# A gated pair of 2-D spectral filters: the last two row transforms on halves of the TensorE array

## The chip, the cores and the metric

The kernel runs on one core of a Trainium2 chip. The metric is the device time of one execution in microseconds. Before the change it is 122.04 us, the median of three runs (122.02 to 122.52).

## The reference

`x` has 2048 rows of 1024 values (bf16). Both branches filter the same `x`; they differ only in their complex weights. The gate is one number for each row.

```python
X = rfft2(x.astype(float32), axes=(-2, -1))          # 2048 x 513, complex
a = irfft2(X * (A_w_r + 1j * A_w_i), s=(2048, 1024)).astype(bfloat16)
b = irfft2(X * (B_w_r + 1j * B_w_i), s=(2048, 1024)).astype(bfloat16)
g = sigmoid((x * gate_w).sum(-1, keepdims=True))
return g * a + (1 - g) * b
```

## The kernel before, in words

All transforms are matmuls with constant matrices. A row transform of length 2048 is done as 32 times 64, a column transform of length 1024 as one real matrix whose symmetry halves the work ("folding": even and odd parts are multiplied apart, and the sum and the difference of the results give the two mirrored halves).

The stages, with the line of their matmul in the profile: stage 1 (L387) does the 32-part of the forward row transform, stage 2 (L456, L465) the forward column transform, stage 4 (L482) the 64-part of the forward row transform. VectorE multiplies by the weights (`product`, L505); the real and imaginary parts of a spectrum sit on alternate partitions, and the copy with the parts swapped is made by a DMA inside SBUF.

Stage 5 (`group_mm`, L614) does the 64-part of the inverse row transform. It works on 256 column indices `l0`, 8 of them in a group. For each, two matmuls (one for each of the tiles WB and WA) accumulate in PSUM: the stationary operand is 128 columns of the products, taken from the tile at a stride of half a slot (264 or 257 elements), so that its columns run slot by slot and, within a slot, over the two halves of the spectrum's columns. The moving operand is a 128-column constant. The result has a PSUM partition for each (slot, half). A group fills two PSUM banks and is copied back to WB in one go, by ScalarE (`group_out`, L625), a few by VectorE (L623). Four pairs of banks are used in turn.

In the middle of stage 5 the gate is made: `row_sums` (VectorE, L533 to L537) ends in AB, `zsum` (L561) spreads AB over the partitions by matmuls, and ScalarE takes the sigmoid (L564). `gate_mask` (L570) then makes two masked copies of the gates, zero on the partitions of the other half, and `rbgen` (L601) multiplies them into the constants of stage 6: 16 row blocks of 1024 elements each on a partition. Twelve of these products are made in stage 5 and four among stages 6 and 7.

Stage 6 (`stage6_mm`, L755) does the 32-part of the inverse row transform and the gated sum of both branches in one contraction over 128 partitions (branch, slot, half). Because the halves must not be mixed, the moving constant has 2 x 32 output columns for every output kind, one set for each half, with zeros where the partition belongs to the other half. A row block takes 16 matmuls of 128 moving columns, and one copy of 1024 columns by ScalarE (L770) to the tile of Y.

Stage 7 (`stage7`, L785) does the inverse column transform of one row block of 128 rows. A folded block takes 8 matmuls of 256 columns; ScalarE copies the even part (L792), VectorE makes sum and difference in f32 (two L832), GpSimd adds and subtracts again and writes bf16 (two L837), and a DMA stores the block. A "full" block uses twice the columns in each matmul (8 of 512) and needs only the copy and two VectorE operations (L796). A "half" block unfolds one part: 4 matmuls of 256 and 4 of 512 columns, four VectorE operations (L818, L796), no GpSimd.

The order of work on each engine is the order of the `P.add` calls; a small planner turns the keys of what is read and written into semaphores, and sets no times. Stage 6 of block r + 2 is issued ahead of stage 7 of block r, with PSUM banks 0 and 1 or 6 and 7 for stage 6 and 2 to 5 for stage 7. Four f32 buffers for VectorE's sums (`NPQ`) stand between it and GpSimd. Stores are issued by SP, two of the last by ScalarE.

Of the kernel before, what the change touches and what calls it, by code (L numbers as in the profile page):

```python
# [6 lines left out]
ALU = mybir.AluOpType  # L7
AP = bass.AP
# [3 lines left out]
RWS = (528, RW)  # L12
# [13 lines left out]
def make_consts():  # L26
# [22 lines left out]
    row = np.arange(128)  # L49
# [4 lines left out]
    F2 = []  # L54
    for cmb, par in ((0, 0), (1, 1), (2, 1), (3, 0)):
# [5 lines left out]
        else:  # L61
            F = F[0].reshape(128, 2, 2, 32, 2)
            e = [np.stack([F[:, :, 0, :, w], F[:, :, 1, :, 1 - w]], axis=2).reshape(128, 128) for w in range(2)]
# [28 lines left out]
    c, s = np.cos(pi2 * kk * o2 / 64), np.sin(pi2 * kk * o2 / 64)  # L92
# [4 lines left out]
    e = np.eye(64)  # L97
# [9 lines left out]
    blocks += [m[perm][:, perm] for m in (T1, T3, -T3, T3z, -T3z, T2, T4, -T4, T4z, -T4z)]  # L107
    C["CL"] = np.concatenate([VR, MK.reshape(128, 64)] + blocks, axis=1)

    l2, sl_, f = row % 2, (row // 2) % 32, row // 64  # L110
    k1 = K1_OF[sl_]
    U5 = np.zeros((128, 16, 2, 2, 4, 32))
    o1 = np.arange(32)[None, :]
# [5 lines left out]
    C["U5"] = U5.reshape(128, 8192)  # L119
    SM = np.zeros((128, 4), np.float32)  # L120
    SM[:, 0] = np.where(f == 0, 1.0, -1.0)
    SM[:, 1], SM[:, 2] = l2 == 0, l2 == 1
    C["SM"] = SM
    DI = np.zeros((128, 2, 2, 2, 512))
    d = np.arange(512)[None, :]
    for pi in range(2):
        for h in range(2):
# [5 lines left out]
            a = pi2 * l * (d + 0.5) / 1024  # L133
# [101 lines left out]
def bass_gated_mix__spectral_gfnet__spectral_gfnet__prompt_kernel(nc, A_x, A_w_r, A_w_i, B_x, B_w_r, B_w_i, gate_w, out):  # L235
# [7 lines left out]
    WA = sb("WA", 64 * RW)  # L243
    WB = sb("WB", 64 * RWS[0])
    FT = sb("FT", 16384)
    XF = sb("XF", 9216)
    MM = sb("MM", 6144)
    F2 = sb("F2", 2048)
    EO = sb("EO", 1024)
    W5 = sb("W5", 64)  # L250
    CK = sb("CK", C["CK"].shape[1])
    CL = sb("CL", C["CL"].shape[1])
# [6 lines left out]
    SM = sb("SM", 4, f32)  # L259
    GRo = 1024  # L260
    DUM = sb("DUM", 2, f32)
    PS = nc.alloc_psum_tensor("PS", [128, 4096], f32)
    WT = (WB, WA)

    def sl(t, off, dims, p0=0, np_=128, pstep=1):
        n = t.shape[1]
        return AP(t, p0 * n + off, [[n * pstep, np_]] + [list(x) for x in dims])

    def ps(col, dims):
        return AP(PS, col, [[4096, 128]] + [list(x) for x in dims])  # L270

    def bank(b):
        return ("ps", b)
# [279 lines left out]
                  r=["XST", "XSS", ("W5", 0), ("W5", 1)], a=["PST"])  # L553


    GMo = lambda r: (XF, 7168 + r * 256) if r < 8 else (MM, 4096 + (r - 8) * 256)

    def zsum(us):
        for k, u in enumerate(us):
            for n in range(16):  # L560
                P.add("pe", lambda e, n=n, u=u, k=k: e.matmul(ps(u * 1024 + 64 * n, [(1, 64)]), sl(AB, 16 * k + n, [(0, 128)]), sl(CL, MKo, [(1, 64)]),  # L561
                                                              start=True, stop=True),
                      r=["AB", "CV"], w=[bank(2 * u + n // 8)])
            P.add("act", lambda e, u=u, k=k: e.activation(sl(XF, 16 * k, [(32, 64), (1, 16)]), ps(u * 1024, [(1, 64), (64, 16)]), ACT.Sigmoid, scale=SM[:, 0:1]),  # L564
                  r=[bank(2 * u), bank(2 * u + 1), "SM"], **({"a" if k else "w": [("CS", 0), ("CS", 1)]}))

    def gate_mask(hf):
        t, o = GMo(8 * hf)
        for h in range(2):
            P.add("dve", lambda e, h=h: e.tensor_scalar(  # L570
                out=sl(t, o + h * 32, [(64, 32), (1, 32)]), in0=sl(XF, 1024 * hf, [(32, 32), (1, 32)]),
                scalar1=SM[:, 1 + h:2 + h], scalar2=None, op0=ALU.mult),
                r=[("CS", hf), "SM"], w=[("GM", hf, h), ("XS" if hf else "X", 4), ("XS" if hf else "X", 5)])


    def col0(u, sw):
# [14 lines left out]
              r=[bank(bk)], w=[("col0", sw)])  # L591

    U5o, DIo = 0, 1024
    RBS = [(FT, (4 + k) * 2048 + 1024, []) for k in range(4)] + [(F2, 1024 * k, ["F2"]) for k in range(2)]
    RBS += [(XF, 1024 * k, [("CS", k)]) for k in range(3)] + [(XF, 3072 + 1024 * k, [("X", k)]) for k in range(4)]
    RBS += [(MM, 1024 * k, [("XS", k)]) for k in range(4)]

    def rbgen(r, eng, after=()):
        t, o, k = RBS[r]
        g, go = GMo(r)  # L600
        return P.add(eng, lambda e: e.tensor_tensor(  # L601
            out=sl(t, o, [(256, 4), (64, 4), (32, 2), (1, 32)]),
            in0=sl(FT, U5o + (r // 2) * 2048 + (r % 2) * 512, [(128, 4), (32, 4), (0, 2), (1, 32)]),
            in1=sl(g, go, [(0, 4), (64, 4), (32, 2), (1, 32)]), op=ALU.mult),
            r=["U5", ("GM", r // 8, 0), ("GM", r // 8, 1)], w=[("RB", r)] + k, after=[last2] + list(after))

    def group_mm(u, g, qs, at):
        hf = g // 16
        for q in qs:
            l0 = 8 * g + q  # L610
            o = ps(u * 1024 + at(q) * 128, [(1, 128)])
            for ab in range(2):
                deps = [("prod", ab, hf, g // 8 % 2), "CL"] + [("col0", ab)] * (g == 0)
                P.add("pe", lambda e, o=o, l0=l0, ab=ab: e.matmul(  # L614
                    o, sl(WT[ab], l0, [(RWS[ab] // 2, 128)]), sl(CL, KIo[ab], [(1, 128)]), start=(ab == 0), stop=(ab == 1)),
                    r=deps, w=[bank(2 * u + at(q) // 4)])

    def group_out(u, g, eng, q0, n, st, at, keys):
        src = ps(u * 1024 + at * 128, [(1, 128), (128, n)])
# [104 lines left out]
    for n, g in enumerate(range(16, 32)):  # L724
        if n == 14:
            last_groups([spare(), spare()])
        elif n < 14:
            group(spare(), g, "dve" if n == 1 else "act")
        if n == 1:
            zsum([spare(), spare()])  # L730
            gate_mask(0)
            gate_mask(1)
            for _ in range(12):
                rbgen(rb.pop(0), "dve")
    assert slots[-2:] == [1, 2]
    last5 = P.ops["pe"][-1]
# [8 lines left out]
    def stage6_mm(r, bs, pis):  # L745
        b0 = 6 * (r % 2)
        t6, o6, _ = RBS[r]
        for b in bs:
            for pi in pis:
                for cp in range(2):  # L750
                    n = cp * 64 + 16 * b + r
                    lh = sl(WB, n * (RWS[0] // 2) + pi, [(2, 128)])
                    rh = sl(t6, o6 + cp * 512 + b * 64, [(256, 2), (1, 64)])
                    o = ps(b0 * 512 + b * 256 + pi * 128, [(1, 128)])
                    P.add("pe", lambda e, o=o, lh=lh, rh=rh, cp=cp: e.matmul(o, lh, rh, start=(cp == 0), stop=(cp == 1)),  # L755
                          r=[("Z", pi), ("RB", r)], w=[bank(b0 + b // 2)])

    def stage6(r, mm=True):
        b0 = 6 * (r % 2)
        if mm:  # L760
            stage6_mm(r, range(4), range(2))
        for k in range(2 if r == 0 else 1):
            n = 2 if r == 0 else 4
            src = ps((b0 + k) * 512, [(32, 8), (1, 32), (256, n)])
            dst = sl(WA, Yo + r * 128 + 2 * k, [(2048, 8), (4, 32), (1, n)])
            kw = dict(r=[bank(b0 + k + q) for q in range(n // 2)], a=[("Y", r)], after=[last5])
            if r == k == 0:
                P.add("dve", lambda e, s=src, d=dst: e.tensor_copy(d, s), **kw)  # L768
            else:
                P.add("act", lambda e, s=src, d=dst: e.activation(d, s, ACT.Copy), **kw)  # L770

    HALF = (5, 9, 12)
    pqc = 0

    def stage7(r):
        nonlocal pqc
        full, half = r >= 14, r in HALF
        b0 = 6 * (r - 14) if r >= 14 else 4 - 2 * (r % 2)
        oo = OUo + (r % NOU) * 1024
        es = sl(WA, EOo + (r % 2) * 1024, [(1, 1024)]).bitcast(f32)  # L780

        def mm(col, c0, n, ri, pi, h, k, last):
            lh = sl(WA, Yo + (pi * 4 + ri * 2 + h) * 2048 + r * 128, [(1, 128)])
            rh = sl(FT, DIo + pi * 2048 + (ri * 2 + h) * 256 + c0 * 4096, [(4096, n), (1, 256)])
            P.add("pe", lambda e: e.matmul(ps(col, [(1, n * 256)]), lh, rh, start=(k == 0), stop=(k == last)),  # L785
                  r=[("Y", r), "DI"] + ["DJ"] * (full or half), w=[bank(col // 512)])
# [14 lines left out]
        if full:  # L801
            for k in range(4):
                mm((b0 + 1) * 512, 0, 2, 1, k // 2, k % 2, k, 3)
            even(0, 512)
            for k0, n, bk in ((0, 2, b0),) if r == 14 else ((0, 1, b0), (1, 1, 4)):
                for k in range(4):
                    mm(bk * 512, k0, n, 0, k // 2, k % 2, k, 3)
                finals(k0, n, bk, WA, EOo + (r % 2) * 1024, [("EO", r % 2)])
        elif half:
# [7 lines left out]
            for s, op in enumerate((ALU.add, ALU.subtract)):  # L817
                P.add("dve", lambda e, s=s, op=op: e.tensor_tensor(out=sl(MM, to + s * 512, [(1, 512)]).bitcast(f32),  # L818
                                                                   in0=ps((b0 + 1) * 512, [(1, 256)]), in1=es[:, :256], op=op),
                      r=[("EO", r % 2), bank(b0 + 1)], w=[("T", r % 2, s), ("GM", 1, 0), ("GM", 1, 1)])  # L820
            finals(0, 2, b0, MM, to, [("T", r % 2, 0), ("T", r % 2, 1)])
        else:
            for e_ in (1, 0):
# [28 lines left out]
    stage6_mm(1, range(2, 4), (0,))  # L852
    stage6_mm(1, range(4), (1,))
    stage6(1, False)
    for _ in range(3):
        rbgen(rb.pop(0), "dve")
    for r in range(16):
        for q in {0: (), 1: (2,), 2: (3, 4)}.get(r, (r + 2,) if r < 14 else ()):
            stage6(q)
        late += stage7(r)  # L860
        if rb:
            rbgen(rb.pop(0), "dve")
        if r < 13:
            outs.append(late.pop()())
    outs += [late[k]() for k in (1, 2, 0, 3)]
# [62 lines left out]
```

## Time and profile before

| | us |
|---|---|
| median of three runs | 122.04 |
| the profiled execution | 122.14 |
| its span | 120.1 |
| PE busy (95% of the span), 1556 matmuls | 114.1 |
| VectorE busy (83%) | 99.5 |
| ScalarE busy (82%) | 99.0 |
| GpSimd busy (32%) | 38.4 |
| stage 5, L614: first start to the last stage 5 matmul | 49.76 to 84.1 |
| stages 6 and 7, L755 and L785 | 84.02 to 115.9 |
| granted TensorE clock, mean | 0.996 |

A PE busy time is the union of pipelined matmul records, each of which lasts longer than its share of the array: a 128-column matmul is shown with 219 ns, while such matmuls start 55.6 ns apart. So the price of a matmul is read from starts, or from the pieces of the chain that ended last, and not from its own duration. Up to 50 us the chain runs over the loading of the weights (SP's queue, 18% of the span; a weight DMA, 9%) and the last products; from there on it is PE for all but the tail.

### The profile page before, as it was taken

Reading aid. Unit: us, or ns where it says so; the run is one execution under the profiler, and the core shown is the slowest. Engines: PE = TensorE matmul, PEld = TensorE weight load, DVE = VectorE, ACT = ScalarE, POOL = GpSimd, SP = SyncE. Lnnn points to the kernel's source line nnn. Section 1 sums busy time; section 2 is a strip of 40 time slices with the busy share of each in tenths; the row PEclk is TensorE's granted clock in tenths of the full one; section 3 lists DMA queues with packets and bytes.
Section 4 is the critical chain, followed back from the end, with each engine's and each line's share of the span. In section 5 each row is a group of like instructions: output and inputs, shape, how many; then the busy total and the mean of one; then the engine's idle time right before and its main releaser. Section 6 shows DMA issues by size and latency. Waiting matters only on the chain.

```text
span 120.1 us, 3690 instructions
## 1 busy us (share of the span) xinstructions
PE 114.1 (95%) x1556; PEld 95.9 (80%) x1556; DVE 99.5 (83%) x160; ACT 99.0 (82%) x119; POOL 38.4 (32%) x47
## 2 busy tenths in 40 slices
PE   6998999999999999999999999999999999999960
PEld 4676889787675675689999999999899979898630
DVE  0568999988999999999999949995695687787890
ACT  4249998999797999899999989999779868867710
POOL 1000010036575500000000000000029999999980
PEclk9999999999999999999999999999999999999998
DMA  2999999999999999832699500000000422434456
GB/s 84 328 394 421 415 331 366 349 350 352 361 369 364 360 370 368 321 137 85 162 392 394 199 0 5 0 5 0 0 5 8 158 96 93 175 124 160 160 222 215
DMA packets 17680, 26.11 MB, mean 217 GB/s; under 512 B 2112, under 2 KB 11072, under 8 KB 17664
## 3 DMA queue, kind: packets, MB, share of 16 engines
q1 hardware_dynamic: 16368, 23.00, 54.6%
q0 software_dynamic: 864, 2.36, 5.4%
q10 hardware_dynamic: 432, 0.52, 1.4%
q8 instruction: 12, 0.20, 0.7%
q14 instruction: 4, 0.03, 0.1%
HBM read 17.48 MB, written 4.19 MB: 180 GB/s over the span
## 4 chain that ended last, share of the span: by engine, by line
PE 59%; SPq 18%; DMA 9%; DVE 8%; issue 3%; ACT 1%; POOL 0%; DVEq 0%; POOLq 0%
PE PS L614 26%; SPq L290 18%; PE PS L785 14%; PE PS L755 11%; DMA WA<-in_B_w_i_dram 9%; DVE WA L505 3%; PE PS L304 3%; DVE WB L505 3%; PE PS L387 2%; DVE WA L796 1%; PE PS L561 1%; PE PS L482 1%; PE PS L588 1%; ACT WB L625 1%; DVEq L867 0%
## 5 line engine op out<-in xcount | busy, mean ns | idle before, releaser
L837 POOL TENSOR_TENSOR WA<-WA 128x512 bf16<-128x512 f32 x22 | 27.6, 1290 | 48.2 <-DVE WA L832 48.2
L614 PE MATMUL PS<-CL,WB 128*128 128x128 bf16 x256 | 31.8, 226 | 0.0
L614 PE MATMUL PS<-CL,WA 128*128 128x128 bf16 x256 | 31.7, 223 | 0.1
L614 PEld LDWEIGHTS PS<-CL,WB 128*128 128x128 bf16 x256 | 31.3, 145 | 0.3 <-DVE WB L505 0.2
L614 PEld LDWEIGHTS PS<-CL,WA 128*128 128x128 bf16 x256 | 31.3, 145 | 0.3 <-DVE WA L505 0.2
L625 ACT ACTIVATE WB<-PS 128x1024 bf16<-128x1024 f32 (+1 forms) x31 | 28.8, 1042 | 0.2 <-PE PS L614 0.2
L770 ACT ACTIVATE WA<-PS 128x1024 bf16<-128x1024 f32 (+1 forms) x16 | 15.8, 996 | 6.2 <-PE PS L755 6.1
L505 DVE TENSOR_TENSOR WB<-XF,WA 128x2048 bf16<-128x2048 bf16 (+2 forms) x14 | 19.3, 1384 | 1.0 <-ACT XF L490 0.5
L785 PE MATMUL PS<-FT,WA 128*128 128x256 bf16 (+1 forms) x132 | 19.3, 292 | 0.1
L505 DVE TENSOR_TENSOR WA<-MM,WA 128x2048 bf16<-128x2048 bf16 (+2 forms) x14 | 19.2, 1385 | 0.0
L482 PE MATMUL PS<-XF,CK 128*128 128x512 bf16 (+1 forms) x72 | 17.5, 356 | 0.2 <-ACT XF L490 0.2
L832 DVE TENSOR_TENSOR WA<-PS,WA 128x512 f32<-128x512 f32 x22 | 14.2, 686 | 4.2 <-PE PS L755 1.9
L471 ACT ACTIVATE XF<-PS 128x1024 bf16<-128x1024 f32 x16 | 16.7, 1052 | 1.1 <-PE PS L465 1.0
L490 ACT ACTIVATE XF<-PS 128x1024 bf16<-128x1024 f32 x14 | 14.7, 1050 | 1.4 <-PE PS L482 0.6
L387 PE MATMUL PS<-MM,XF 128*128 128x256 bf16 x128 | 15.4, 280 | 0.3 <-DVE XF L348 0.3
L387 PEld LDWEIGHTS PS<-MM,XF 128*128 128x128 bf16 x128 | 12.5, 100 | 3.3 <-DVE XF L348 1.4
L785 PEld LDWEIGHTS PS<-FT,WA 128*128 128x128 bf16 x132 | 12.3, 98 | 3.3 <-DVE WA L768 0.2
L290 POOL DMA_DIRECT2D MM<-XF x18 | 9.9, 550 | 14.3 <-PE PS L482 8.7
L398 ACT ACTIVATE FT<-PS 128x1024 bf16<-128x1024 f32 (+2 forms) x15 | 13.1, 1012 | 0.9 <-PE PS L387 0.9
L348 DVE TENSOR_TENSOR XF<-WB 128x512 bf16<-128x512 bf16 (+1 forms) x20 | 6.0, 366 | 5.9 <-DMA WB<-in_A_x_dram 5.9
L456 PEld LDWEIGHTS PS<-F,FT 128*128 128x128 bf16 x128 | 8.4, 98 | 3.1 <-ACT FT L398 0.2
L456 PE MATMUL PS<-F,FT 128*128 128x128 bf16 x128 | 10.2, 219 | 0.0
(77 smaller groups left out, 134.1 us busy)
## 6 DMA issues: line engine op xcount, KB each, us to landing
out_dram<-WA SPq DMA_DIRECT2D x14, 256.0 KB, 2.2
MM<-XF POOLq DMA_DIRECT2D x18, 128.0 KB, 5.3
WA<-in_A_x_dram SPq DMA_DIRECT2D x4, 512.0 KB, 8.3
FT<-c_U SPq DMA_DIRECT2D x1, 2048.0 KB, 8.5
MM<-XF SPq DMA_DIRECT2D x14, 128.0 KB, 3.2
WB<-in_A_x_dram SPq DMA_DIRECT2D x3, 512.0 KB, 5.9
WA<-in_A_w_r_dram SPq DMA_DIRECT2D x4, 256.5 KB, 5.8
WA<-in_A_w_i_dram SPq DMA_DIRECT2D x4, 256.5 KB, 6.2
```

The costliest lines, as they stand in the source:

```text
L290: return P.add(eng, lambda e: e.dma_start(dst, src), dma=name, **kw)
L387: P.add("pe", lambda e, o=o, lh=lh, rh=rh, s=s: e.matmul(o, lh, rh, start=(s == 0), stop=(s == 1)), r=[("xf", c % 2, q, h, s ^ j), ("M", c ...
L456: P.add("pe", lambda e, o=o, cs=cs, j=j, t=t, rh=rh: e.matmul(o, fblock(1 + cs, j, t), rh, start=(j == 0), stop=(j == 1)), r=[("F1a" if p ...
L471: P.add("act", lambda e: e.activation(dst, src, ACT.Copy), **kw)
L482: P.add("pe", lambda e, o=o, kind=kind, pm=pm, m=m, rh=rh: e.matmul(o, sl(CK, fbo(kind, pm, m), [(1, 128)]), rh, start=(m == 0), stop=(m = ...
L490: P.add("act", lambda e: e.activation(dst, src, ACT.Copy), **kw)
L505: P.add("dve", lambda e: e.tensor_tensor(out=at(sw), in0=sl(xt, xo + 64 * h0, [(0, 2), (128, 8 * ni), (1, 64 * n)]), in1=at(1), op=ALU.mul ...
L614: P.add("pe", lambda e, o=o, l0=l0, ab=ab: e.matmul(o, sl(WT[ab], l0, [(RWS[ab] // 2, 128)]), sl(CL, KIo[ab], [(1, 128)]), start=(ab == 0) ...
L625: P.add("act", lambda e: e.activation(dst, src, ACT.Copy), r=b, a=keys)
L770: P.add("act", lambda e, s=src, d=dst: e.activation(d, s, ACT.Copy), **kw)
L785: P.add("pe", lambda e: e.matmul(ps(col, [(1, n * 256)]), lh, rh, start=(k == 0), stop=(k == last)), r=[("Y", r), "DI"] + ["DJ"] * (full o ...
L837: P.add("pool", lambda e, s=s, op=op: e.tensor_tensor(out=ods(s, 0, 2), in0=pv[:, :, 0, :], in1=pv[:, :, 1, :], op=op), r=[("PQ", pk, 0), ...
```

## The change

- Stage 5: each matmul of 128 stationary columns becomes two of 64 (one half of the spectrum's columns each), at twice the stride. The first writes PSUM partitions 0 to 63, the second 64 to 127. The partitions of the result now run over (half, branch, slot).
- Stage 6: each matmul becomes two, with the partitions 0 to 63 (one half) and 64 to 127 (the other) of both operands. The moving operand has 64 columns instead of 128; the two write different PSUM banks.
- The constants of stage 6 are 512 elements a partition instead of 1024, hold no zeros, and need no masked gates: `gate_mask` goes, and all 16 `rbgen` follow `zsum` in stage 5, into tiles that are free by then.
- Stage 7: blocks 4 and 9 are full, as 14 and 15 were; blocks 2, 7 and 12 are half, instead of 5, 9 and 12. The layout of Y and the first copies of stage 6 follow the new banks.

```diff
-    l2, sl_, f = row % 2, (row // 2) % 32, row // 64
+    sl_, f = row % 32, row // 32 % 2
...
-    def gate_mask(hf):
-        t, o = GMo(8 * hf)
-        for h in range(2):
-            P.add("dve", lambda e, h=h: e.tensor_scalar(
-                out=sl(t, o + h * 32, [(64, 32), (1, 32)]), in0=sl(XF, 1024 * hf, [(32, 32), (1, 32)]),
-                scalar1=SM[:, 1 + h:2 + h], scalar2=None, op0=ALU.mult),
...
+    RBS = [(FT, (4 + k // 2) * 2048 + 1024 + 512 * (k % 2), []) for k in range(8)] + [(F2, 512 * k, ["F2"]) for k in range(4)]
+    RBS += [(XF, 2048 + 512 * k, [("CS", 2)]) for k in range(2)] + [(XF, 3072 + 512 * k, [("X", 0)]) for k in range(2)]
...
-            out=sl(t, o, [(256, 4), (64, 4), (32, 2), (1, 32)]),
-            in0=sl(FT, U5o + (r // 2) * 2048 + (r % 2) * 512, [(128, 4), (32, 4), (0, 2), (1, 32)]),
-            in1=sl(g, go, [(0, 4), (64, 4), (32, 2), (1, 32)]), op=ALU.mult),
+            out=sl(t, o, [(128, 4), (1, 128)]), in0=sl(FT, U5o + (r // 2) * 2048 + (r % 2) * 512, [(128, 4), (1, 128)]),
+            in1=sl(XF, r * 128, [(0, 4), (1, 128)]), op=ALU.mult), r=["U5", "GM"], w=[("RB", r)], a=k, after=[last2] + list(after))
...
-                P.add("pe", lambda e, o=o, l0=l0, ab=ab: e.matmul(
-                    o, sl(WT[ab], l0, [(RWS[ab] // 2, 128)]), sl(CL, KIo[ab], [(1, 128)]), start=(ab == 0), stop=(ab == 1)),
+                for h in range(2):
+                    o = AP(PS, 64 * h * 4096 + u * 1024 + at(q) * 128, [[4096, 64], [1, 128]])
+                    P.add("pe", lambda e, o=o, l0=l0, ab=ab, h=h: e.matmul(
+                        o, sl(WT[ab], l0 + RWS[ab] // 2 * h, [(RWS[ab], 64)]), sl(CL, KIo[ab], [(1, 128)]), start=(ab == 0), stop=(ab == 1)),
...
-            gate_mask(0)
-            gate_mask(1)
-            for _ in range(12):
+            for _ in range(16):
                 rbgen(rb.pop(0), "dve")
...
-                    lh = sl(WB, n * (RWS[0] // 2) + pi, [(2, 128)])
-                    rh = sl(t6, o6 + cp * 512 + b * 64, [(256, 2), (1, 64)])
-                    o = ps(b0 * 512 + b * 256 + pi * 128, [(1, 128)])
+                    for h in range(2):
+                        lh = sl(WB, n * (RWS[0] // 2) + pi, [(2, 128)], p0=64 * h, np_=64)
+                        rh = sl(t6, o6 + cp * 256 + b * 32, [(128, 2), (1, 32)], p0=64 * h, np_=64)
+                        o = ps((b0 + h) * 512 + pi * 256 + b * 32, [(128, 2), (1, 32)])
...
-            n = 2 if r == 0 else 4
-            src = ps((b0 + k) * 512, [(32, 8), (1, 32), (256, n)])
-            dst = sl(WA, Yo + r * 128 + 2 * k, [(2048, 8), (4, 32), (1, n)])
+            n = 4 if r == 0 else 8
+            src = ps((b0 + k) * 512, [(128, n), (1, 32), (32, 4)])
+            dst = sl(WA, Yo + k * 8192 + r * 128, [(2048, n), (4, 32), (1, 4)])
...
-    HALF = (5, 9, 12)
+    HALF, FULL = (2, 7, 12), (4, 9, 14, 15)
...
-        full, half = r >= 14, r in HALF
+        full, half = r in FULL, r in HALF
...
-    for _ in range(3):
-        rbgen(rb.pop(0), "dve")
...
-        if rb:
-            rbgen(rb.pop(0), "dve")
```

More of the change, by code (lines that the diff above doesn't have):

```diff
@@ L121, in make_consts @@
     SM[:, 0] = np.where(f == 0, 1.0, -1.0)
-    SM[:, 1], SM[:, 2] = l2 == 0, l2 == 1
     C["SM"] = SM
@@ L553, in star_products @@
                   r=["XST", "XSS", ("W5", 0), ("W5", 1)], a=["PST"])
-    GMo = lambda r: (XF, 7168 + r * 256) if r < 8 else (MM, 4096 + (r - 8) * 256)
     def zsum(us):
@@ L564, in zsum @@
             P.add("act", lambda e, u=u, k=k: e.activation(sl(XF, 16 * k, [(32, 64), (1, 16)]), ps(u * 1024, [(1, 64), (64, 16)]), ACT.Sigmoid, scale=SM[:, 0:1]),
-                  r=[bank(2 * u), bank(2 * u + 1), "SM"], **({"a" if k else "w": [("CS", 0), ("CS", 1)]}))
-    def gate_mask(hf):
-        t, o = GMo(8 * hf)
-        for h in range(2):
-            P.add("dve", lambda e, h=h: e.tensor_scalar(
-                out=sl(t, o + h * 32, [(64, 32), (1, 32)]), in0=sl(XF, 1024 * hf, [(32, 32), (1, 32)]),
-                scalar1=SM[:, 1 + h:2 + h], scalar2=None, op0=ALU.mult),
-                r=[("CS", hf), "SM"], w=[("GM", hf, h), ("XS" if hf else "X", 4), ("XS" if hf else "X", 5)])
+                  r=[bank(2 * u), bank(2 * u + 1), "SM"], a=["GM"], **({} if k else {"w": [("CS", 0), ("CS", 1)]}))
     def col0(u, sw):
@@ L593, in bass_gated_mix__spectral_gfnet__spectral_gfnet__prompt_kernel @@
     U5o, DIo = 0, 1024
-    RBS = [(FT, (4 + k) * 2048 + 1024, []) for k in range(4)] + [(F2, 1024 * k, ["F2"]) for k in range(2)]
-    RBS += [(XF, 1024 * k, [("CS", k)]) for k in range(3)] + [(XF, 3072 + 1024 * k, [("X", k)]) for k in range(4)]
-    RBS += [(MM, 1024 * k, [("XS", k)]) for k in range(4)]
+    RBS = [(FT, (4 + k // 2) * 2048 + 1024 + 512 * (k % 2), []) for k in range(8)] + [(F2, 512 * k, ["F2"]) for k in range(4)]
+    RBS += [(XF, 2048 + 512 * k, [("CS", 2)]) for k in range(2)] + [(XF, 3072 + 512 * k, [("X", 0)]) for k in range(2)]
     def rbgen(r, eng, after=()):
         t, o, k = RBS[r]
-        g, go = GMo(r)
         return P.add(eng, lambda e: e.tensor_tensor(
-            out=sl(t, o, [(256, 4), (64, 4), (32, 2), (1, 32)]),
-            in0=sl(FT, U5o + (r // 2) * 2048 + (r % 2) * 512, [(128, 4), (32, 4), (0, 2), (1, 32)]),
-            in1=sl(g, go, [(0, 4), (64, 4), (32, 2), (1, 32)]), op=ALU.mult),
-            r=["U5", ("GM", r // 8, 0), ("GM", r // 8, 1)], w=[("RB", r)] + k, after=[last2] + list(after))
+            out=sl(t, o, [(128, 4), (1, 128)]), in0=sl(FT, U5o + (r // 2) * 2048 + (r % 2) * 512, [(128, 4), (1, 128)]),
+            in1=sl(XF, r * 128, [(0, 4), (1, 128)]), op=ALU.mult), r=["U5", "GM"], w=[("RB", r)], a=k, after=[last2] + list(after))
     def group_mm(u, g, qs, at):
@@ L610, in group_mm @@
             l0 = 8 * g + q
-            o = ps(u * 1024 + at(q) * 128, [(1, 128)])
             for ab in range(2):
                 deps = [("prod", ab, hf, g // 8 % 2), "CL"] + [("col0", ab)] * (g == 0)
-                P.add("pe", lambda e, o=o, l0=l0, ab=ab: e.matmul(
-                    o, sl(WT[ab], l0, [(RWS[ab] // 2, 128)]), sl(CL, KIo[ab], [(1, 128)]), start=(ab == 0), stop=(ab == 1)),
-                    r=deps, w=[bank(2 * u + at(q) // 4)])
+                for h in range(2):
+                    o = AP(PS, 64 * h * 4096 + u * 1024 + at(q) * 128, [[4096, 64], [1, 128]])
+                    P.add("pe", lambda e, o=o, l0=l0, ab=ab, h=h: e.matmul(
+                        o, sl(WT[ab], l0 + RWS[ab] // 2 * h, [(RWS[ab], 64)]), sl(CL, KIo[ab], [(1, 128)]), start=(ab == 0), stop=(ab == 1)),
+                        r=deps, w=[bank(2 * u + at(q) // 4)])
     def group_out(u, g, eng, q0, n, st, at, keys):
@@ L751, in stage6_mm @@
                     n = cp * 64 + 16 * b + r
-                    lh = sl(WB, n * (RWS[0] // 2) + pi, [(2, 128)])
-                    rh = sl(t6, o6 + cp * 512 + b * 64, [(256, 2), (1, 64)])
-                    o = ps(b0 * 512 + b * 256 + pi * 128, [(1, 128)])
-                    P.add("pe", lambda e, o=o, lh=lh, rh=rh, cp=cp: e.matmul(o, lh, rh, start=(cp == 0), stop=(cp == 1)),
-                          r=[("Z", pi), ("RB", r)], w=[bank(b0 + b // 2)])
+                    for h in range(2):
+                        lh = sl(WB, n * (RWS[0] // 2) + pi, [(2, 128)], p0=64 * h, np_=64)
+                        rh = sl(t6, o6 + cp * 256 + b * 32, [(128, 2), (1, 32)], p0=64 * h, np_=64)
+                        o = ps((b0 + h) * 512 + pi * 256 + b * 32, [(128, 2), (1, 32)])
+                        P.add("pe", lambda e, o=o, lh=lh, rh=rh, cp=cp: e.matmul(o, lh, rh, start=(cp == 0), stop=(cp == 1)),
+                              r=[("Z", pi), ("RB", r)], w=[bank(b0 + h)])
     def stage6(r, mm=True):
@@ L762, in stage6 @@
         for k in range(2 if r == 0 else 1):
-            n = 2 if r == 0 else 4
-            src = ps((b0 + k) * 512, [(32, 8), (1, 32), (256, n)])
-            dst = sl(WA, Yo + r * 128 + 2 * k, [(2048, 8), (4, 32), (1, n)])
-            kw = dict(r=[bank(b0 + k + q) for q in range(n // 2)], a=[("Y", r)], after=[last5])
+            n = 4 if r == 0 else 8
+            src = ps((b0 + k) * 512, [(128, n), (1, 32), (32, 4)])
+            dst = sl(WA, Yo + k * 8192 + r * 128, [(2048, n), (4, 32), (1, 4)])
+            kw = dict(r=[bank(b0 + k + q) for q in range(n // 4)], a=[("Y", r)], after=[last5])
             if r == k == 0:
@@ L782, in mm @@
         def mm(col, c0, n, ri, pi, h, k, last):
-            lh = sl(WA, Yo + (pi * 4 + ri * 2 + h) * 2048 + r * 128, [(1, 128)])
+            lh = sl(WA, Yo + (h * 4 + pi * 2 + ri) * 2048 + r * 128, [(1, 128)])
             rh = sl(FT, DIo + pi * 2048 + (ri * 2 + h) * 256 + c0 * 4096, [(4096, n), (1, 256)])
@@ L804, in stage7 @@
             even(0, 512)
-            for k0, n, bk in ((0, 2, b0),) if r == 14 else ((0, 1, b0), (1, 1, 4)):
+            for k0, n, bk in ((0, 2, b0),) if r < 15 else ((0, 1, b0), (1, 1, 4)):
                 for k in range(4):
@@ L819, in stage7 @@
                                                                    in0=ps((b0 + 1) * 512, [(1, 256)]), in1=es[:, :256], op=op),
-                      r=[("EO", r % 2), bank(b0 + 1)], w=[("T", r % 2, s), ("GM", 1, 0), ("GM", 1, 1)])
+                      r=[("EO", r % 2), bank(b0 + 1)], w=[("T", r % 2, s), ("XS", 4), ("XS", 5)])
             finals(0, 2, b0, MM, to, [("T", r % 2, 0), ("T", r % 2, 1)])
```

## The prediction

> **What bounds the kernel now.** I read the chain that ended last first, then the pitch of each kind of matmul, then what the other engines have left beside TensorE. By the page, PE carries 59% of the chain. In order of time, these are the pieces of it from the point at which stage 5 is half done (start us, us, what):
>
> ```profile
> 69.50 0.93 PE PS L561 x32
> 70.43 13.67 PE PS L614 x224
> 84.12 0.76 ACT WB L625
> 84.92 1.29 PE PS L755 x20
> 86.28 1.03 PE PS L785 x8
> 87.31 0.89 PE PS L755 x16
> 88.20 0.87 PE PS L785 x8
> ...
> 96.17 1.30 PE PS L785 x8
> ...
> 111.58 3.48 PE PS L785 x20
> ```
>
> The reader is to see pitches. A stage 5 pair (weight load and 128-column matmul, L614) costs 13.67/224 = 61.0 ns, a stage 6 pair (L755, also 128 columns) 0.89/16 = 55.6 ns, and a 64-column pair (L561) 0.93/32 = 29.1 ns. Stage 7 of a row block costs 0.87 us when folded, 1.30 us when half unfolded, and a full block 3.48 - 0.87 (block 13, folded) over 12 matmuls = 0.218 each, so 8 x 0.218 = 1.74 us. The smallest pair in the trace has 2 columns: eight (L518) start at 26.67, the next line starts at 26.87, 25 ns each:
>
> ```profile
> 26.67 0.34 PE L518 MATMUL PS<-CK,FT 128*128 128x2 bf16 x8
> 26.87 1.02 PE L482 MATMUL PS<-XF,CK 128*128 128x512 bf16 x4
> ```
>
> Now what lies beside PE. Stage 5 on ScalarE and VectorE, then one normal block of stages 6 and 7 on ScalarE, then the end of GpSimd (start, us, engine, line, what, idle before):
>
> ```profile
> 68.88 0.18 DVE L537 CAST AB<-AT 128x32 bf16<-128x32 f32 x1
> 72.01 11.95 ACT L625 ACTIVATE WB<-PS 128x1024 bf16<-128x1024 f32 x13
> 92.67 1.02 ACT L770 ACTIVATE WA<-PS 128x1024 bf16<-128x1024 f32 x1 [0.23 <-PE PS L755]
> 93.59 0.59 ACT L792 ACTIVATE WA<-PS 128x512 f32<-128x512 f32 x1
> 94.44 1.02 ACT L770 ACTIVATE WA<-PS 128x1024 bf16<-128x1024 f32 x1 [0.26 <-PE PS L755]
> 89.24 25.07 POOL L837 TENSOR_TENSOR WA<-WA 128x512 bf16<-128x512 f32 x20 [47.85 <-DVE WA L832]
> ```
>
> ScalarE evacuates a stage 5 group in 11.95/13 = 0.92 us, where PE makes one in 16 x 61.0 = 0.98. In a normal block it needs 94.18 - 92.67 = 1.51 us and then waits 0.26 for PE, whose block is 0.89 + 0.87 = 1.76. GpSimd never pauses from 89.24 to 114.31, 1.25 us an operation, two for each folded block. So PE sets the pace, and everything else is close behind it.
>
> **Stage 5.** 512 pairs of 128 weight columns become 1024 pairs of 64 weight columns with the same 128 moving columns, each into one half of the PSUM partitions. No row shows a matmul on half the array: every group on the page says 128*128. So the price of two halves is bounded: 55.6 ns if both stream at once at the pitch of L755, 2 x 55.6 = 111 if they go one after the other. What L614 adds to L755 is its weight load (145 ns against 98), from columns far apart; the two halves load the same 128 columns from the same addresses in sum. I therefore take the row that it is nearest to, L614 itself: **61 ns for two halves, no change**. A gain is capped anyhow. Before the zsum matmuls (L561), PE has to wait for AB, ready at 69.06, and they start at 69.33, so the first half can give 0.27 us; after them ScalarE's 0.92 against 0.98 caps 14 groups at 0.8. Together at most 1.1.
>
> **Stage 6.** 16 pairs of 128 x 128 become 32 pairs with 64 rows of contraction and 64 moving columns. The half of the moving columns that multiplied zeros is gone. One after the other, that is 32 x 29.1 = 0.93 us a block, 0.04 more than now. With both row halves at once it is 16 x 29.1 = 0.47. A bound between them is the 25 ns of the 2-column pairs: 32 x 25 = 0.80, if that is the rate at which PE can start pairs at all. I take **0.47**: the halves use different rows, different PSUM banks and different partitions of both operands, so that nothing which the rows show to cost time (moving columns) is shared. [...]
>
> **Stage 7.** Blocks 4 and 9 become full; 2, 7 and 12 are half instead of 5, 9 and 12. Of blocks 0 to 13, 9 are folded, 3 half, 2 full: 9 x 0.87 + 3 x 1.30 + 2 x 1.74 = 15.2 us, against 11 x 0.87 + 3 x 1.30 = 13.5 now. That is 1.7 us **more** on PE. In exchange GpSimd does 18 operations, not 22: 18 x 1.25 = 22.5 us.
>
> **VectorE, off the path.** Sixteen L601 at 0.68 (10.9 us) and four L570 at 0.5 (2.0) go; sixteen products of 512 elements come, at most 0.42 each by the 128x512 row of L443: 6.7 us from 72.2, done by 79, with its next evacuation at 82.67 as cover. If that cover failed, the first row constants are late for 84.02, and each us late is a us of PE. Four L601 that stood between stage 6 and the first sums of stage 7 go as well, which brings GpSimd's start forward by a few tenths.
>
> **The sum.** Now: stage 7 starts at 86.28, blocks 0 to 13 take 14 x 0.89 + 13.5 = 26.0 (the trace: 26.2, to 112.45, so 0.2 of gaps). After: the 20 pairs from 84.92 become 40 at half the price, which puts the first evacuation some 0.3 earlier, start 85.95. PE then needs 14 x 0.47 + 15.2 = 21.8. But a folded block would be 0.47 + 0.87 = 1.34 on PE and is 1.51 on ScalarE, so 9 x 0.17 = 1.5 is lost: 23.3, and 0.2 of gaps, end at 109.45. Gain 3.0 us. GpSimd, started near 88, has 22.5 us of work and is free at about 110.5, before its last two operations become ready (109.45 + 0.59 + 1.3 = 111.3). VectorE has 9 x 1.29 + 3 x 2.1 + 2 x 1.29 = 20.5, less than 23.3. Blocks 14 and 15 and the stores behind them stay. The profiled execution took 122.14 us (span 120.1, 2.0 around it), so **122.14 - 3.0 = 119.1**; the median of the three runs is 0.1 lower, which I leave inside the rounding.
>
> **Rivals.**
> 1. *Halves don't overlap in stage 6.* 14 x 0.93 + 15.2 = 28.2, start 86.3, end 114.7: 2.3 us later, **124.4**. For it: no row shows two matmuls sharing the array, and busy matmul records overlap only as a pipeline. At the 25 ns floor: 14 x 0.80 + 15.2 + 0.2 from 86.2, end 112.8, 0.3 later, **122.5**.
> 2. *Every change between whole and half array empties the pipeline.* A 128-column matmul lasts 219 ns where pairs go at 55.6, so up to 164 ns are in flight. Two changes a block, 28 in all, 4.6 us on the 21.8: end 112.6, **122.2**, all of the gain eaten. Up to 0.08 a change would vanish in ScalarE's 0.17 of a folded block. The present trace alternates L755 and L785 with no gap, but both are whole-array matmuls, so it cannot speak on this. [...]
> 3. *Halves don't overlap in stage 5* (the other side, and far). 512 x (111 - 61) = 25.7 us, of which stage 6 gives 3.0 back: **144.8**. It decides from 61 + 3.0/0.512 = 67 ns for two halves, for stage 5 has no other slack: PE stands at busy 6.00 of 6.00 us there. For it: both halves use the same rows of the array, and their weights come from strided columns, the load that already costs most. Against it: their columns and PSUM partitions are apart. [...]
>
> **Chances.** Forecast, with a visible gain (118 to 121.4): 0.51. Rival 2 or the 25 ns floor, fully or in part (121 to 123): 0.17. Rival 1 without any overlap, alone or with rival 2 (124 to 129): 0.12. Rival 3 (over 129): 0.20. What a measurement can tell from no change is about 0.5%, 0.6 us. Of the 0.17, 0.02 lies below 121.4 and 0.03 above 122.7: faster 0.53, same 0.12, slower 0.35. The range goes from the forecast with all of stage 5's cap (119.1 - 1.1 = 118.0) to rival 1 with rival 2's full price (124.4 + 4.6 = 129.0) and leaves out only rival 3.
>
> **What would show it.** Right: a stage 6 piece of the chain near 0.47 us for 32 matmuls; ScalarE without idle time in the folded blocks, waiting on PE only in full ones; a stage 5 piece of 448 matmuls near 13.7 us; PE at the end of block 13 near 109.5. Wrong: 0.8 to 0.93 in stage 6 (rival 1), a gap of 0.1 or more wherever the stage 6 line and the stage 7 line meet (rival 2), a stage 5 group above 1.07 us on PE with ScalarE waiting for it (rival 3).

## The result, and the profile after

| | before | after |
|---|---|---|
| median, us | 122.07 | 151.84 |
| ratio to before (95% interval) | 1 | 1.2435 (1.240 to 1.247) |
| span of the profiled execution, us | 120.1 | 149.8 |
| first stage 5 matmul to first stage 6 matmul, us | 49.76 to 84.02: 34.3 | 49.8 to 115.39: 65.6 |
| first stage 6 matmul to the end of the last stage 7 matmul, us | 84.02 to 115.92: 31.9 | 115.39 to 145.64: 30.25 |

Of the runs of one kernel, those more than 1.5% above its fastest are left out of the times and ratios in this document. The kernel became 29.8 us slower. Stage 5 lost 31.3 us, stages 6 and 7 won 1.65, and 31.3 - 1.65 is the 29.7 us between the spans. Everything ahead of stage 5 stayed.

The chain view of the new page breaks off after the last 1.5 us, so the stages are read from groups and from PE's timeline. First the page's groups: weight load of stage 5 before, then its matmul, its load and its evacuation after (line, engine, operation, tiles, shape, count | busy us, mean ns | idle before, releaser):

```profile
L614 PEld LDWEIGHTS PS<-CL,WB 128*128 128x128 bf16 x256 | 31.3, 145 | 0.3 <-DVE WB L505 0.2
```

```profile
L600 PE MATMUL PS<-CL,WB 128*64 128x128 bf16 x512 | 62.1, 285 | 0.0
...
L600 PEld LDWEIGHTS PS<-CL,WB 128*64 128x64 bf16 x512 | 58.1, 217 | 0.9 <-DVE WB L504 0.4
...
L611 ACT ACTIVATE WB<-PS 128x1024 bf16<-128x1024 f32 (+1 forms) x31 | 31.2, 1007 | 27.9 <-PE PS L600 27.9
```

Each load brings half as many columns and takes longer, 217 ns instead of 145, and ScalarE now sits idle for 27.9 us behind PE. PE's timeline in stage 5 after (start us, us):

```profile
99.82 0.29 PE L600 MATMUL PS<-CL,WA 128*64 128x128 bf16 x2
99.94 0.30 PE L600 MATMUL PS<-CL,WB 128*64 128x128 bf16 x2
100.06 0.29 PE L600 MATMUL PS<-CL,WA 128*64 128x128 bf16 x2
```

Every row holds the matmuls of both tiles. Two of them, at 283 to 285 ns each, fit in 0.29 to 0.30, so they start within some 10 ns of each other: the tiles **do** work side by side. But a new two start only every 120 ns, where the whole array took 61. Stages 6 and 7 after:

```profile
128.56 1.05 PE L770 MATMUL PS<-FT,WA 128*128 128x256 bf16 x8
129.53 0.64 PE L740 MATMUL PS<-F,WB 64*128 64x64 bf16 x32
130.11 1.47 PE L770 MATMUL PS<-FT,WA 128*128 128x256 bf16 x8
131.51 0.64 PE L740 MATMUL PS<-F,WB 64*128 64x64 bf16 x32
132.09 1.05 PE L770 MATMUL PS<-FT,WA 128*128 128x256 bf16 x8
```

From start to start, 32 half-array matmuls take 0.58 us (0.89 before for 16 whole ones), a folded block 0.97 (0.87), a half block 1.40 (1.30). About 0.10 us is lost at each change between half and whole array. ScalarE in a folded block, after:

```profile
128.69 1.02 ACT L755 ACTIVATE WA<-PS 128x1024 bf16<-128x1024 f32 x1
129.61 0.59 ACT L777 ACTIVATE WA<-PS 128x512 f32<-128x512 f32 x1
130.24 1.02 ACT L755 ACTIVATE WA<-PS 128x1024 bf16<-128x1024 f32 x1
```

It goes from one copy to the next without the 0.25 us that it waited before: 1.55 us a block, which is also PE's 0.58 + 0.97. PE takes the same time in the folded block that starts at 132.09 (to 133.64), although ScalarE had just waited 0.68 us for it. So the 1.55 us is PE's own pace, changes included, and ScalarE's 1.51 lies just below it.

### The profile page after: what moved, and what is told of

It reads as the page before. It is cut to its first block, busy times and chain, and to the rows that moved or that the text cites. A ratio compares the mean times of both kernels' runs of the same rounds, so it can differ in the third digit from the quotient of the medians.

```text
span 149.8 us, 5218 instructions
## 1 busy us (share of the span) xinstructions
PE 143.1 (96%) x2324; PEld 119.5 (80%) x2324; DVE 93.3 (62%) x156; ACT 101.7 (68%) x119; POOL 33.5 (22%) x43
## 5 line engine op out<-in xcount | busy, mean ns | idle before, releaser
L600 PE MATMUL PS<-CL,WB 128*64 128x128 bf16 x512 | 62.1, 285 | 0.0
L600 PE MATMUL PS<-CL,WA 128*64 128x128 bf16 x512 | 61.9, 283 | 0.0
L600 PEld LDWEIGHTS PS<-CL,WB 128*64 128x64 bf16 x512 | 58.1, 217 | 0.9 <-DVE WB L504 0.4
L600 PEld LDWEIGHTS PS<-CL,WA 128*64 128x64 bf16 x512 | 57.9, 216 | 0.1
L611 ACT ACTIVATE WB<-PS 128x1024 bf16<-128x1024 f32 (+1 forms) x31 | 31.2, 1007 | 27.9 <-PE PS L600 27.9
L822 POOL TENSOR_TENSOR WA<-WA 128x512 bf16<-128x512 f32 x18 | 22.5, 1280 | 82.9 <-DVE WA L817 82.7
L609 DVE CAST WB<-PS 128x512 bf16<-128x512 f32 (+1 forms) x3 | 2.7, 906 | 36.4 <-PE PS L600 36.4
L770 PE MATMUL PS<-FT,WA 128*128 128x256 bf16 (+1 forms) x132 | 21.1, 306 | 0.4 <-DVE WA L753 0.4
L481 PE MATMUL PS<-XF,CK 128*128 128x512 bf16 (+1 forms) x72 | 17.5, 356 | 0.2 <-ACT XF L489 0.2
L770 PEld LDWEIGHTS PS<-FT,WA 128*128 128x128 bf16 x132 | 11.8, 98 | 5.6 <-DVE WA L753 0.5
L817 DVE TENSOR_TENSOR WA<-PS,WA 128x512 f32<-128x512 f32 x18 | 11.6, 685 | 4.5 <-PE PS L740 3.0
```

What stands on the lines that cost most here:

```text
L481: P.add("pe", lambda e, o=o, kind=kind, pm=pm, m=m, rh=rh: e.matmul(o, sl(CK, fbo(kind, pm, m), [(1, 128)]), rh, start=(m == 0), stop=(m = ...
L600: P.add("pe", lambda e, o=o, l0=l0, ab=ab, h=h: e.matmul(o, sl(WT[ab], l0 + RWS[ab] // 2 * h, [(RWS[ab], 64)]), sl(CL, KIo[ab], [(1, 128)] ...
L611: P.add("act", lambda e: e.activation(dst, src, ACT.Copy), r=b, a=keys)
L822: P.add("pool", lambda e, s=s, op=op: e.tensor_tensor(out=ods(s, 0, 2), in0=pv[:, :, 0, :], in1=pv[:, :, 1, :], op=op), r=[("PQ", pk, 0), ...
```

## The experiments

Theory L, after reading the trace: the two column tiles overlap, but the load of 64 far columns into one tile takes 120 ns, and that is the pitch. Rival M: the two matmuls take turns at some 60 ns. Rival L2: the loads take turns at 60.

### Stage 5 alone undone

```diff
-                for h in range(2):
-                    o = AP(PS, 64 * h * 4096 + u * 1024 + at(q) * 128, [[4096, 64], [1, 128]])
-                        o, sl(WT[ab], l0 + RWS[ab] // 2 * h, [(RWS[ab], 64)]), ...
+                o = ps(u * 1024 + at(q) * 128, [(1, 128)])
+                    o, sl(WT[ab], l0, [(RWS[ab] // 2, 128)]), ...
```

> The changed kernel with the stage 5 matmuls of before (128 stationary columns at once). It leaves the rows of stage 5 in the old order, so that stage 6 adds up the wrong rows: only its time counts. If the two column tiles of stage 5 are all of the loss, stage 5 is back at 61 ns for each l0 and tile (34.3 us instead of 65.5 from its first matmul to stage 6), and what stages 6 and 7 won in the trace (30.25 us from the first stage 6 matmul to the last of stage 7, against 31.9) is left: about 120.4 us. Rival: with stage 5 fast, the evacuations of ScalarE collide with the start of stage 6 and nothing is left of the 1.65: 122.

Measured: 120.99 us, ratio 0.9896 (0.983 to 0.997). Stage 6 begins at 84.27, and it is 30.25 us again to the end of stage 7. So the column tiles of stage 5 are the whole of the loss, and the rest of the change is worth a little over 1 us.

### The new block lists alone, on the kernel before

```diff
-    HALF = (5, 9, 12)
+    HALF, FULL = (2, 7, 12), (4, 9, 14, 15)
...
-        full, half = r >= 14, r in HALF
+        full, half = r in FULL, r in HALF
...
-            for k0, n, bk in ((0, 2, b0),) if r == 14 else ...
+            for k0, n, bk in ((0, 2, b0),) if r < 15 else ...
```

> The kernel before with the new lists of full and half blocks alone (4 and 9 full, 2, 7 and 12 half). If PE alone sets the pace of stages 6 and 7 there, the 1.7 us of added stage 7 matmuls come in full: 123.8. Rival: the relief of GpSimd (18 operations instead of 22) and of VectorE pays for it: 122.1 or less.

Measured: 124.07 us, ratio 1.0135 (1.009 to 1.018), some 1.6 us. The stretch of stages 6 and 7 grew by 1.7 us (84.27 to 117.87). PE alone set the pace there, and the relief of GpSimd was worth nothing by itself; it takes the faster stage 6 to make use of it.

### One tile of the two

```diff
-                for h in range(2):
+                for h in range(1):
```

> The changed kernel with only the first of the two column halves in stage 5 (half of the stage 5 products is left out). Theory L, loads: each 64-column load takes 120 ns by itself, and the loads of the two tiles ran beside each other, so leaving out one saves nothing: about 120 ns for one matmul, 152 us. Theory L2: the loads of the two tiles go one after the other, 60 each, so that one alone takes 60: 120 us. Theory M, streams in turn: the matmuls of the two tiles went one after the other at some 60 ns each, so that one alone takes 56 to 61: 120 us.

Measured: 151.55 us. Half of the matmuls gone, and no time with them. PE's timeline of that run:

```profile
55.78 0.28 PE L600 MATMUL PS<-CL,WB 128*64 128x128 bf16 x1
55.90 0.28 PE L600 MATMUL PS<-CL,WA 128*64 128x128 bf16 x1
56.01 0.29 PE L600 MATMUL PS<-CL,WB 128*64 128x128 bf16 x1
```

One matmul each 120 ns. M and L2 both fall: neither streams nor loads of the two tiles took turns.

### Half of the moving columns

```diff
-[[4096, 64], [1, 128]]) ... sl(CL, KIo[ab], [(1, 128)])
+[[4096, 64], [1, 64]]) ... sl(CL, KIo[ab], [(1, 64)])
```

> The changed kernel with 64 moving columns instead of 128 in every stage 5 matmul (half of the stage 5 products is left out). Theories L and L2: the loads set the pitch, so that nothing changes: 120 ns for the two halves, 152 us. Theory M: the matmuls take turns and are half as long, 2 x 29 = 58 ns: about 120 us.

Measured: 153.3 us. The granted clock fell to about a half from some 58 us on (see the last section), and at half the clock theory M would ask for 2 x 58 = 116 ns, too near to 120 to be told from it. So only the start of stage 5 decides, at a granted clock of 1.00. PE's timeline there:

```profile
50.26 0.29 PE L600 MATMUL PS<-CL,WB 128*64 128x64 bf16 x2
50.38 0.29 PE L600 MATMUL PS<-CL,WA 128*64 128x64 bf16 x2
50.50 0.29 PE L600 MATMUL PS<-CL,WB 128*64 128x64 bf16 x2
```

Two matmuls start every 120 ns, as with 128 moving columns: their length did not matter. The same cut in the kernel before:

> The kernel before with 64 moving columns in stage 5 (half of the stage 5 products is left out). Theory L: the 61 ns there are the load of 128 far columns, four groups of 32 at once, so nothing changes: 61 ns a pair, 122 us. Rival: they belong to the matmul, and the pair falls towards the 29 ns of the other 64-column pairs; the evacuations of ScalarE then set stage 5 at 0.92 us a group: 121.

Measured: 122.23 us, 60 ns from matmul to matmul. So the 61 ns of stage 5 before belonged to the load of its 128 far columns as well, and not to the matmul that was on it in the chain.

### How far the columns are apart

The stationary operand came from a constant with its columns at a chosen distance:

```diff
-sl(WT[ab], l0 + RWS[ab] // 2 * h, [(RWS[ab], 64)])
+sl(CL, 64 * h + ab, [(1, 64)])     # s5_cl1
+sl(CL, ab, [(4, 64)])              # s5_cl4
+sl(CL, ab, [(32, 64)])             # s5_cl32
```

With 4 and with 32 elements both halves load the same columns.

> The changed kernel with the stationary columns of stage 5 taken from 64 adjacent columns of a constant (the products are left out of stage 5). If it is the distance between columns that makes a load slow, the pair falls to what its matmul needs, 56 to 61 ns: about 121 us. If a half-array load is slow whatever the distance: 120 ns, 152 us.

> As the kernels with the stationary columns of stage 5 from a constant, at a distance of 4 elements (8 bytes; the products are left out of stage 5). Adjacent columns gave 110 ns a load and 57 ns for two, 64 bytes 204 ns and 110 for two. If every distance but 1 (and the 2 of stage 6) is slow: 110 ns for two, 148 us. If the price grows with the distance, or sets in between 8 and 64 bytes: about 57 for two, 123 us.

> As the kernel with adjacent columns, but with columns 32 elements (64 bytes) apart (the products are left out of stage 5 here too; both halves load the same columns). If distance alone counts and 64 bytes are far: 120 ns, 152 us, as for the 1056 and 1028 bytes of the changed kernel. If the slow load comes only from columns many hundred bytes apart: 56 to 61 ns, 121 us.

Measured: 123.44, 125.76 and 147.97 us. PE's timeline after the zsum matmuls, first with adjacent columns, then with 8 bytes between them:

```profile
73.79 12.70 PE L600 MATMUL PS<-CL 128*64 128x128 bf16 x448
```

```profile
75.72 13.67 PE L600 MATMUL PS<-CL 128*64 128x128 bf16 x448
```

That is 56.7 and 61.0 ns for two halves (a little too much, for the length of the last matmul is in it). With 64 bytes it is 2 x 15.0/274 = 109 ns (274 matmuls in the 15 us from 60 to 75). The loads last 110, 145, 204 and, at the kernel's 1028 and 1056 bytes, 217 ns. In these runs the price grew with the distance, and at 64 bytes it was nearly that of the kernel's own. With adjacent columns the tiles are as fast as predicted. The first two runs still stand above 121. PE had idle time in stage 5 (3.5 and 1.9 us, "issue"), to which the next experiment speaks; with 8 bytes the granted clock also fell to 0.54 to 0.61 between 68 and 72 us, where 160 matmuls took 6.39 us, 80 ns for two. That leaves more than 1 us of the 125.76 unexplained.

### Four tiles of 32 columns

If a tile's load costs its number of columns and tiles load side by side, four tiles would do 128 columns in the time of 32.

```diff
-                for h in range(2):
-                    o = AP(PS, 64 * h * 4096 + ..., [[4096, 64], [1, 128]])
-                        o, sl(WT[ab], l0 + RWS[ab] // 2 * h, [(RWS[ab], 64)]), ...
+                for h in range(4):
+                    o = AP(PS, 32 * h * 4096 + ..., [[4096, 32], [1, 128]])
+                        o, sl(WT[ab], l0 + RWS[ab] // 2 * (h // 2) + 32 * RWS[ab] * (h % 2), [(RWS[ab], 32)]), ...
```

> The changed kernel with four column tiles of 32 in stage 5 instead of two of 64 (each half once more by branch; the partitions of the result stay as they are). Theory L: the load of a tile costs its number of strided columns, 120/64 = 1.87 ns each, and the tiles load beside each other. Then four loads of 32 columns take 60 ns together, stage 5 is back at some 34 us, and the kernel at the time of the run with whole-array stage 5, 121.0. Rival L3: all tiles share one path of 0.94 ns a column (one tile alone took 120 for another reason): 120 for the four, 152 us. Rival: PE cannot start pairs of load and matmul fast enough (25 ns each, as its smallest pairs did): 100 for the four, some 142 us.

Measured: 148.58 us, ratio 1.214 (1.206 to 1.222). The forecast of 121 fell, but not on the loads. PE's timeline where it runs, and then its matmul group on the page:

```profile
57.83 0.26 PE L600 MATMUL PS<-CL,WB 128*32 128x128 bf16 x4
57.89 0.26 PE L600 MATMUL PS<-CL,WA 128*32 128x128 bf16 x4
57.96 0.27 PE L600 MATMUL PS<-CL,WB 128*32 128x128 bf16 x2
```

```profile
L600 PE MATMUL PS<-CL,WB 128*32 128x128 bf16 x1024 | 39.1, 239 | 18.6 <-issue 18.5
```

Four tiles take some 64 ns while they run (28 rows of four start between 59.37 and 61.10), as theory L has it. But PE stands idle for 19.5 us of stage 5 and waits for nothing that the profile shows. (A smaller part is lost to the granted clock, which was 0.50 from 70 to 74 us.) The gaps come regularly (from 88 us on they end at 90.48, 93.93, 97.93 and 101.66), and the DMA view has a queue that grew with them, here and in the kernel before:

```profile
q8 instruction: 26, 0.43, 1.2%
```

```profile
q8 instruction: 12, 0.20, 0.7%
```

PE's loads and matmuls are 6696 here and 3112 before, so both have one packet (16 KB) for every 256 of them (26.2 and 12.2); the changed kernel has 18 for 4648. Stage 5 here has 4096 in 62.8 us, 15.3 ns each or 3.9 us for 256, which is about the distance of the gaps. And PE runs exactly one packet between two gaps, as the windows around three bursts show (us | length, PE busy and count, PEld busy and count, then the other engines):

```profile
90.40:93.00 2.60, 2.31 (x128) 2.17 (x128) 2.60 (x8) 2.13 (x3) 0.00 (x0) 1.00 0.02 6
93.90:97.00 3.10, 2.31 (x128) 2.17 (x128) 1.95 (x6) 1.85 (x2) 0.00 (x0) 1.00 0.03 5
97.90:100.50 2.60, 2.30 (x128) 2.16 (x128) 0.00 (x0) 1.38 (x2) 0.00 (x0) 1.00 0.03 6
```

128 matmuls and 128 loads are 256 instructions. These gaps fall where the DMA engines are almost free (share 0.02 to 0.03); the longest one, 3.8 us up to 68.94, falls where data transfers filled them (1.05 from 65 to 69 us), as do the 1.9 us with 8 bytes (1.03) and the first of the two gaps with adjacent columns (1.02). The test of it was the same small tiles with few instructions:

> The four-tile kernel with only the first of its four tiles in stage 5 (three quarters of the stage 5 products are left out). Theory L: a load of 32 far columns takes 60 ns by itself; stage 5 is back at some 34 us, with no idle time of PE, since PE gets half as many instructions as with two tiles: about 121 us. Rival: the 20 us of idle time in the four-tile run come from the small tiles themselves and not from the number of instructions: then gaps of 1 to 4 us stay in stage 5, 130 us or more.

Measured: 122.0 us, one matmul every 61 ns, and no gap in the waits of PE's matmuls. So a load of 32 far columns takes at most 61 ns alone, and the small tiles do not cause the gaps. (Whole-array pairs with 128 moving columns and near weights start 55.6 ns apart, so the 61 can be partly the matmul's and bounds the load from above. The record of the load is 145 ns, as for the 128 far columns on the whole array, where the load did set the 61; no run had shorter matmuls on the small tile.) That PE's instructions were not brought in faster than some 15 ns each is what the packets and the gaps fit; no run changed their supply, so it is an inference.

### Fewer changes between half and whole array

```diff
-        for q in {0: (), 1: (2,), 2: (3, 4)}.get(r, (r + 2,) if r < 14 else ()):
+        for q in (r + 1, r + 2) if r % 2 and r < 14 else ():
```

> The kernel with whole-array stage 5 (rows of stage 5 in the old order, so that stage 6 adds up the wrong rows), with stage 6 of two blocks issued together: 14 changes between half and whole array instead of 27. If the 0.1 us of each change is on the path: 1.3 us less than 121.0, 119.7. Rival: ScalarE already sets the folded blocks (1.55 us a block without idle time): 121.0 or more.

> As the four-tile kernel, with stage 6 of two row blocks issued together (blocks r + 1 and r + 2 ahead of stage 7 of every odd r), so that PE changes between half and whole array 14 times instead of some 27. If the 0.1 us of each change is on the path, 13 x 0.1 = 1.3 us less than the four-tile kernel. Rival: ScalarE sets the folded blocks already (1.55 us a block, no idle time), and its copies then come in bunches: the same time or more.

Measured: 120.77 us, ratio 0.985 (0.978 to 0.992), against 0.9896 (0.983 to 0.997) for the same kernel without pairs; and on four tiles 147.18 and 148.14 us (two runs) against 148.58 (147.91 to 150.12). The 1.3 us were not shown: the intervals overlap, and in the traces of both paired kernels the stretch of stages 6 and 7 is some 29.85 us instead of 30.25. PE's timeline, then ScalarE's, around blocks 10 and 11 of the paired run with whole-array stage 5:

```profile
105.10 1.11 PE L739 MATMUL PS<-XF,WB 64*128 64x64 bf16 x64
106.14 2.35 PE L769 MATMUL PS<-FT,WA 128*128 128x256 bf16 x16
108.42 1.11 PE L739 MATMUL PS<-XF,WB 64*128 64x64 bf16 x64
```

```profile
105.81 1.94 ACT L754 ACTIVATE WA<-PS 128x1024 bf16<-128x1024 f32 x2 [0.45 <-PE PS L739]
107.63 0.88 ACT L776 ACTIVATE WA<-PS 128x512 f32<-128x512 f32 x2
```

Stage 6 of two blocks takes 1.04 us, one change less. But the 16 matmuls of two folded blocks take 2.28 us from start to start, where 2 x 0.87 is their work: ScalarE first makes both copies of stage 6, and the even part comes after them. The two blocks cost 3.32 us, 1.66 each, against 1.55 unpaired; what the other blocks win is nearly given back. In the unpaired folded block ScalarE's 1.51 us lies 0.04 below PE's 1.55, so that fewer changes could win almost nothing there; in the pairs the order on ScalarE costs more than that. This is read from the traces, and a difference of a few tenths of a microsecond cannot be settled by these intervals.

## Why the prediction was wrong

The forecast was 119.1 us (118.0 to 129.0). It is **wrong**, by one term.

**The step that failed** is the price of stage 5: "61 ns for two halves, no change". The row it was taken from was the right one to look at, the weight load of L614 (145 ns against 98); it was read wrongly. I argued that the two halves load the same 128 columns "in sum", and so cost the same. What the runs showed in its place: in one tile, 64 far columns take 120 ns and 32 at most 61, some 1.9 ns a column, whatever the other tiles do; on the whole array 128 far columns take 61 (also with 64 moving columns, so it is the load), as much as 32 in a tile. By these two prices, an estimate, the whole array is as fast as four groups of 32 at once would be. Two tiles of 64 load side by side and still need the time of 64 columns each. So the halves doubled the price: 512 x (120 - 61) = 30.2 us of the 31.3 by which stage 5 grew. Most of the rest is a term that the prediction left out: in stage 5 too PE changes to whole-array work and back, four times, and each time costs 0.2 to 0.3 us (four matmuls of L481 at 54.39 take 0.96 us from start to start instead of 0.86, with 0.23 us in front of them where two halves take 0.12). The trace of before had no load into a part of the array, so that nothing in it showed what a narrower one costs. The load of 128 columns (145 ns, against 98 from near ones) was slow for the distance of its columns and still fast for its width, 61 ns for 128 columns where a tile takes 120 for 64, and the change took the second away.

**The rivals.** Rival 3 named the place and the threshold (67 ns for two halves), and it came true, at a chance of 0.20. Its mechanism was wrong: the halves do overlap, within 10 ns. Only the ground it gave beside that, the loads from strided columns, was the right one. Its price was too low by some 7 us, 144.8 against 151.84, for matmuls in turn would have cost 111 ns and not 120, stages 6 and 7 gave back 1.65 instead of 3.0, and the changes inside stage 5 cost about 1 us. Rival 1 is refuted: 32 half-array pairs take 0.47 us and the change to stage 7. Rival 2 is right in that each change costs time, 0.10 us and not its bound of 0.164; that the pipeline is emptied there, no run shows.

**Stage 6** was right: 0.47, as predicted, next to the 0.10 of a change. **Stages 6 and 7 together**: forecast 3.0 us, measured 1.65, and 1.65 again with stage 5 undone. The difference is the changes: a folded block took 1.55 us instead of 1.51, since ScalarE's copies hide most of them (9 x 0.04 = 0.4), but the five half and full blocks show them in full, 5 x 0.2 = 1.0. **Stage 7's lists**: 1.7 us of PE work forecast, 1.7 measured by themselves. **VectorE**: the sixteen shorter products were done at 95.6, long before the copy that needed VectorE next at 112.63; their cover held. **Stage 5's cap** of 1.1 us of gain was never reached: where two tiles were as fast as 56.7 ns, with adjacent columns, PE stood idle for 3.5 us without a wait that the profile shows.

**What stays open.** The rest of the change is worth about 1.3 us (1.0% of the time, by the interval 0.3 to 1.7%) in a kernel whose stage 5 uses the whole array, but that one computes something else. To have both, the products would have to lie half by half, so that one stride runs over the slots of one half and then of the other. The weights come in rows of 513, and each would have to be loaded in two pieces, while SP's queue at some 0.6 us an issue already makes 18% of the chain. This was not tried, and no kernel that does all of the work was found to beat the one before.

## What to carry to other kernels

Here the split over array tiles was free only in what it streams: two tiles took 56.7 ns with adjacent columns and 120 ns with far ones. Ask the price of the weight load of one tile by itself, in columns and in their distance, before the overlap of tiles is counted as a gain; row tiles kept their loads short here (95 ns with 128 columns, 4 bytes apart), column tiles of far columns did not (217 ns with 64 columns); no run had row tiles with far columns. And count instructions: with 6696 loads and matmuls in the kernel instead of 3112, PE stood idle for 19.5 us of stage 5 without a wait that the profile shows, most likely short of instructions; no run changed their supply.

## What the runs showed that was not expected

- With 64 moving columns on two tiles, the granted clock fell to about a half in stage 5, and the pitch stayed: 336 matmuls in 20 us are 119 ns for two, against 120 at the full clock. The windows of that run (us | length, PE busy and count, PEld, DVE, ACT, POOL, granted clock, DMA share, GB/s):

```profile
70.00:90.00 20.00, 20.00 (x336) 19.77 (x335) 1.23 (x1) 10.63 (x12) 0.00 (x0) 0.52 0.01 2
```

  So the load of far columns did not go at the pace of that clock here (0.52 in these 20 us). Why the clock fell is open: the kernel before with the same cut kept 0.993. It also fell for a few microseconds in the run with 8 bytes and in the one with four tiles, each time behind a long gap of PE (1.9 and 3.8 us); here no such gap came first.
- Four small tiles start a load and a matmul every 16 ns while they run, less than the 25 ns of the smallest whole-array pairs, so that those 25 ns were no limit on how fast PE takes its instructions here. Over the whole of stage 5 they had one instruction every 15.3 ns, and each pair is two.
